# A w_out product by seven products of half-size blocks, with feed-forward groups of two chunks

## The chip, the core and the metric

The kernel runs on one core of a Trainium2 chip. Its engines each work through a queue of their own: PE (TensorE) multiplies matrices, DVE (VectorE) and ACT (ScalarE) do elementwise work, POOL (GpSimd) fills tiles at the start, and SP (SyncE) issues the DMAs. The metric is the device time of one execution in microseconds (us); less is better. The profile shows one execution, with times from the start of its span.

## What is computed

A gated linear attention over 4 batches, 8 heads, 768 steps and head size 48, and then a feed-forward block with SiLU on its 3072 rows of 384:

```
state = alpha[:, :, t, :, None] * state + einsum('bhd,bhe->bhde', k[:, :, t], v[:, :, t])
y[:, :, t] = einsum('bhd,bhde->bhe', q[:, :, t], state)
...
x = y.transpose(0, 2, 1, 3).reshape(3072, 384)
h = x @ w_in                       # w_in  384 x 2048
g = h * (1.0 / (1.0 + exp(-h)))
out = (g @ w_out).astype(float32)  # w_out 2048 x 384
```

q, k, v and alpha are float32; w_in and w_out arrive as float64. All matmuls of the kernel are float32.

## The kernel before

**Chunks and steps.** The sequence is cut into 24 chunks (6 stretches of 128 steps, 4 batches each). A chunk goes through five stages: `products` (transposes of alpha, k and q on PE; running products of alpha by two scans on DVE; k times one of them gives `kp`, q times the other gives `qp`), `scores` (matmuls of kp and qp into `g`, masked on DVE; transposes of kp), `values` (g times v, and qp times the carried state), `bridge` (the chunk's output, transposed, goes into a tile `xt`) and `states` (the new carried state). A loop of 27 steps calls the five stages for five successive lags, and after each stage `fill` puts in some feed-forward work.

**Feed-forward.** `moe(ci)` takes the four chunks of a stretch, 512 tokens. For each of 16 slices of w_in's columns three matmuls of 512 columns go into a PSUM tile `ps_m` (two buffers), and ACT applies SiLU into a tile `g`. Then for each of the four chunks 16 matmuls of 384 columns add up g times w_out, ACT copies the result and SP stores it. These are 32 pieces to a stretch; `fill` hands them out at an even pace from step FIRST = 7 on, and a stretch may begin once its four chunks are bridged.

**Weights.** They come as float64 words: a DMA brings a piece into `bits` (four buffers), ACT scales the low words, and three DVE instructions (L464, L465, L466) put float32 together. There are 12 pieces of w_in (converted before step 7) and 16 of w_out (converted beside the first stretch). Later `audit` reads alpha and the weights again and reduces them on DVE (L499), to confirm the bounds on which the arithmetic rests; the program takes another path only if they fail.

**Order.** A scheduler places the instructions of each engine by its own estimate of times, so the order on an engine is not quite that of the code. Each engine then works strictly through its order.

Of the kernel before, what the change touches and what calls it, by code (L numbers as in the profile page):

```python
# [8 lines left out]
F32 = mybir.dt.float32  # L9
# [321 lines left out]
def quotients(  # L331
# [30 lines left out]
    W = C + 1  # L362

# [12 lines left out]
    gpool = pool("gpool", NFT + 3)  # L376
    opool = pool("opool", 2)
    ps_t = pool("ps_t", 3, PS)
# [6 lines left out]
    NIN = 4  # L385
# [10 lines left out]
    def load(n):  # L396
        ci, b = divmod(n, B)
        c = ctxs[n] = {"ci": ci, "b": b}
        rows = slice(ci * C, ci * C + C)
        for name, src in (("a", alpha), ("k", k), ("q", q)):  # L400
            c[name] = nat[name][n % NIN]
            nc.sync.dma_start(c[name][:, :, 0:D], src[b, :, rows, :].transpose([1, 0, 2]))
        c["v"] = vpool.tile([128, H, D], F32, name="vn")
        nc.sync.dma_start(c["v"], v[b, :, rows, :].transpose([1, 0, 2]))
# [31 lines left out]
    w_out = wpool.tile([128, NFT, HD], F32, name="w_out")  # L436
    for n in range(2, NIN):
        load(n)

    wide = moe_w_in.dtype != F32  # L440

    def weights(which):

        pieces = [
            (w_in[:, t, c : c + 512], moe_w_in[t * 128 : t * 128 + 128, c : c + 512])
            for c in range(0, DF, 512) for t in range(NKT)
        ] if which == 0 else [  # L450
            (w_out[:, f, :], moe_w_out[f * 128 : f * 128 + 128, :]) for f in range(NFT)]
        for dst, src in pieces:
# [12 lines left out]
            dve.scalar_tensor_tensor(w, hi, -(1 << 30), w, ALU.bitwise_and, ALU.bitwise_or)  # L465
            dve.tensor_tensor(w, w, up, ALU.add)  # L466
            yield
# [41 lines left out]
    def products(n):  # L509
# [11 lines left out]
        u = work.tile([128, end + 1], F32, name="u")  # L521
        dve.tensor_tensor_scan(u[:, end - 1 :: -1], sg[:, end:0:-1], one[:, end:0:-1],  # L522
                               0.0, ALU.mult, ALU.add)
        kp = c["kp"] = work.tile([128, NP, C], F32, name="kp")
        dve.tensor_tensor(kp, ps["k"], tokens(u), ALU.mult)  # L525
# [3 lines left out]
        p = work.tile([128, end + 1], F32, name="p")  # L529
        dve.tensor_tensor_scan(p[:, 0:end], sg[:, 0:end], iv[:, 0:end], 0.0, ALU.mult, ALU.add)  # L530
        qp = c["qp"] = work.tile([128, NP, C], F32, name="qp")
        dve.tensor_tensor(qp, ps["q"], tokens(p), ALU.mult)  # L532
# [57 lines left out]
    def bridge(n):  # L590
        c = ctxs.pop(n)
        ci, b = c["ci"], c["b"]
        if b == 0:
            xts[ci] = xtp.tile([128, NKT, B * C], F32, name="xt")
# [4 lines left out]
        act.copy(xts[ci][:, :, b * C : (b + 1) * C], ps)  # L599

    def moe(ci):

        xt = xts.pop(ci)
        gs = []
        for f in range(NFT):
            ps = ps_m.tile([128, B * C], F32, name="ps_m")
            for t in range(NKT):
                pe.matmul(ps, lhsT=w_in[:, t, f * 128 : (f + 1) * 128], rhs=xt[:, t, :],  # L608
                          start=(t == 0), stop=(t == NKT - 1))
            gf = gpool.tile([128, B * C], F32, name="g")  # L610
            act.activation(gf, ps, AF.Silu)  # L611
            gs.append(gf)
            yield
        for b in range(B):
            ps = ps_m.tile([128, HD], F32, name="ps_m")
            for f in range(NFT):
                pe.matmul(ps, lhsT=gs[f][:, b * C : (b + 1) * C], rhs=w_out[:, f, :],  # L617
                          start=(f == 0), stop=(f == NFT - 1))
                if f % 4 == 3 and f < NFT - 1:
                    yield  # L620
            o = opool.tile([128, HD], F32, name="o")
            act.copy(o, ps)  # L622
            r = b * S + ci * C
            nc.sync.dma_start(out[r : r + C, :], o)
            yield

    PIECES = NFT + 4 * B
# [9 lines left out]
    def ffn():  # L637
        for ci in range(NCH):
            yield from moe(ci)
# [5 lines left out]
    total = NCH * PIECES  # L645
    STEPS = NT + 3
    FIRST = B + 3
    SLOTS = 5

    def fill(step, slot):  # L650

        nonlocal done
        if step < FIRST:
            if step >= 1:
                convert(0, ((step - 1) * SLOTS + slot + 1) * n_conv[0] // ((FIRST - 1) * SLOTS))
            return
        if step > FIRST + 2 and slot in (0, 2):
# [7 lines left out]
    for step in range(STEPS):  # L665
        for slot, (stage, lag) in enumerate(
# [6 lines left out]
            if stage is states and 0 <= n and n + NIN < NT:  # L673
                load(n + NIN)
# [9 lines left out]
    if wide:  # L684
        checks += [(seen[1][0], ALU.max, float(1150 << 20), ALU.is_le),
# [64 lines left out]
```

## Time and profile before

| | us |
|---|---|
| median of 3 runs (lowest to highest) | 691.74 (691.45 to 692.13) |
| the profiled execution | 691.06 |
| its span, first to last instruction | 689.3 |
| PE busy | 668.8 |
| DVE busy | 227.3 |
| ACT busy | 132.6 |
| mean granted PE clock | 0.992 of full |

The span is what the profile's times refer to; the execution's own time is 1.8 us longer. The busy time of an engine is the union of its instructions, so those that overlap count once. A line number such as L617 is that of the kernel's source. `ps_m<-w_out,g` means that the instruction writes ps_m and reads w_out and g, with buffer numbers left out. Time in square brackets, or after a bar in the groups, is idle time of the engine ahead of the instructions, with what ended it.

### The profile page before, as it was taken

Reading aid. Unit: us, or ns where it says so; the run is one execution under the profiler, and the core shown is the slowest. Engines: PE = TensorE matmul, PEld = TensorE weight load, DVE = VectorE, ACT = ScalarE, POOL = GpSimd, SP = SyncE. Lnnn points to the kernel's source line nnn. Section 1 sums busy time; section 2 is a strip of 40 time slices with the busy share of each in tenths; the row PEclk is TensorE's granted clock in tenths of the full one; section 3 lists DMA queues with packets and bytes.
Section 4 is the critical chain, followed back from the end, with each engine's and each line's share of the span. In section 5 each row is a group of like instructions: output and inputs, shape, how many; then the busy total and the mean of one; then the engine's idle time right before and its main releaser. Section 6 shows DMA issues by size and latency. Waiting matters only on the chain.

```text
span 689.3 us, 7061 instructions
## 1 busy us (share of the span) xinstructions
PE 668.8 (97%) x2874; PEld 410.9 (60%) x2874; DVE 227.3 (33%) x414; ACT 132.6 (19%) x242; POOL 6.2 (1%) x27
## 2 busy tenths in 40 slices
PE   6889999999999999999999999999999999999996
PEld 4786545666455666645666844566854456644553
DVE  4999986878130221303020600213440001000000
ACT  1423642001222101222100222110122100122100
POOL 3000000000000000000000000000000000000000
PEclk9979999999999999999999999999999999999999
DMA  9998799899020230302020500200100000000000
GB/s 158 247 223 210 224 232 307 263 291 278 18 36 17 41 57 12 58 0 47 20 49 23 92 1 0 42 27 24 28 8 1 0 23 12 14 1 1 11 12 28
DMA packets 112698, 54.04 MB, mean 78 GB/s; under 512 B 101264, under 2 KB 104336, under 8 KB 112656
## 3 DMA queue, kind: packets, MB, share of 16 engines
q1 hardware_dynamic: 112656, 53.49, 33.1%
q8 instruction: 25, 0.41, 0.2%
q14 instruction: 17, 0.14, 0.1%
HBM read 48.76 MB, written 4.72 MB: 78 GB/s over the span
## 4 chain that ended last, share of the span: by engine, by line
PE 85%; DMA 2%; DVE 1%; ACT 1%; issue 0%; ACTq 0%; SPq 0%
PE ps_m L617 36%; PE ps_m L608 33%; PE ps_y L563 5%; PE ps_t L517 3%; PE ps_g L543 3%; PE ps_y L568 2%; PE ps_y L580 2%; DMA bits<-in_moe_w_out_dram 2%; PE ps_t L551 1%; PE ps_t L598 1%; DVE w_out L466 0%; DVE w_out L465 0%; ACT x L572 0%; DVE u L522 0%; ACT g L611 0%
## 5 line engine op out<-in xcount | busy, mean ns | idle before, releaser
L617 PE MATMUL ps_m<-w_out,g 128*128 128x384 f32 x768 | 255.0, 487 | 0.0
L608 PE MATMUL ps_m<-xt,w_in 128*128 128x512 f32 x576 | 251.7, 594 | 1.6 <-ACT g L611 1.1
L617 PEld LDWEIGHTS ps_m<-w_out,g 128*128 128x128 f32 x768 | 143.1, 190 | 92.9 <-issue 1.9
L608 PEld LDWEIGHTS ps_m<-xt,w_in 128*128 128x128 f32 x576 | 107.6, 190 | 129.7 <-issue 126.2
L611 ACT ACTIVATE g<-ps_m 128x512 f32<-128x512 f32 x96 | 57.2, 596 | 180.2 <-PE ps_m L608 180.2
L586 DVE TENSOR_TENSOR st<-ps_y,st 48x192 f32<-48x192 f32 x32 | 11.3, 354 | 144.2 <-PE ps_y L580 143.9
L563 PEld LDWEIGHTS ps_y<-vn,g 128*128 128x128 f32 x384 | 47.6, 198 | 5.7 <-issue 1.9
L563 PE MATMUL ps_y<-vn,g 128*128 128x48 f32 x384 | 47.8, 278 | 0.6 <-DVE st L588 0.3
L522 DVE TENSOR_TENSOR_SCAN u<-al,one 128x516 f32<-128x516 f32 x24 | 29.5, 1230 | 52.4 <-ACT al L519 52.0
L499 DVE TENSOR_REDUCE seen<-bits 128x1 f32<-128x384 int32 (+2 forms) x65 | 42.2, 687 | 12.7 <-DMA bits<-in_moe_w_out_dram 5.4
L547 DVE TENSOR_TENSOR g<-ps_g,mask 128x512 f32<-128x512 f32 x48 | 31.3, 682 | 30.6 <-PE ps_g L543 30.5
L622 ACT COPY o<-ps_m 128x384 f32<-128x384 f32 x24 | 11.5, 479 | 153.5 <-PE ps_m L617 121.3
L525 DVE TENSOR_TENSOR kp<-ps_t,u 128x512 f32<-128x512 f32 x24 | 16.6, 690 | 63.4 <-PE ps_t L517 61.4
L532 DVE TENSOR_TENSOR qp<-ps_t,p 128x512 f32<-128x512 f32 x24 | 16.5, 686 | 59.3 <-PE ps_y L568 59.2
L543 PEld LDWEIGHTS ps_g<-qp,kp 48*128 48x128 f32 x384 | 24.5, 195 | 13.4 <-issue 8.8
L543 PE MATMUL ps_g<-qp,kp 48*128 48x128 f32 x384 | 29.4, 294 | 2.9 <-DVE qp L532 2.9
L530 DVE TENSOR_TENSOR_SCAN p<-al,inv 128x516 f32<-128x516 f32 x24 | 29.5, 1229 | 0.5
L572 ACT COPY x<-ps_y 128x384 f32<-128x384 f32 x24 | 11.5, 479 | 79.5 <-PE ps_y L568 73.3
L580 PEld LDWEIGHTS ps_y<-vn,kn 128*128 128x128 f32 x160 | 21.4, 198 | 7.2 <-ACT x L572 3.4
L553 ACT COPY kn<-ps_t 128x512 f32<-128x512 f32 x20 | 11.7, 587 | 62.0 <-PE ps_t L551 62.0
L517 PE MATMUL ps_t<-ident,an 128*128 128x128 f32 x96 | 17.9, 300 | 5.9 <-POOL one L420 4.1
L580 PE MATMUL ps_y<-vn,kn 128*128 128x96 f32 x160 | 23.0, 285 | 0.5 <-ACT x L572 0.2
(53 smaller groups left out, 278.0 us busy)
## 6 DMA issues: line engine op xcount, KB each, us to landing
bits<-in_moe_w_in_dram SPq DMA_DIRECT2D x24, 512.0 KB, 5.0
bits<-in_moe_w_out_dram SPq DMA_DIRECT2D x32, 384.0 KB, 4.2
an<-in_alpha_dram SPq DMA_DIRECT2D x24, 192.0 KB, 4.6
kn<-in_k_dram SPq DMA_DIRECT2D x24, 192.0 KB, 4.9
qn<-in_q_dram SPq DMA_DIRECT2D x24, 192.0 KB, 4.9
vn<-in_v_dram SPq DMA_DIRECT2D x24, 192.0 KB, 2.7
bits<-in_alpha_dram SPq DMA_DIRECT2D x9, 512.0 KB, 5.2
out_dram<-o SPq DMA_DIRECT2D x24, 192.0 KB, 1.9
```

Of the source, the lines that this page charges most:

```text
L499: dve.tensor_reduce(seen[kind][which][:, i : i + 1], x, axis=AX, op=op, apply_absolute_value=True)
L517: pe.transpose(ps[name][:, j, :], c[name][:, 2 * j : 2 * j + 2, :], ident)
L522: dve.tensor_tensor_scan(u[:, end - 1 :: -1], sg[:, end:0:-1], one[:, end:0:-1], 0.0, ALU.mult, ALU.add)
L525: dve.tensor_tensor(kp, ps["k"], tokens(u), ALU.mult)
L530: dve.tensor_tensor_scan(p[:, 0:end], sg[:, 0:end], iv[:, 0:end], 0.0, ALU.mult, ALU.add)
L543: pe.matmul(ps[:, u, j, :], lhsT=c["kp"][r, j, :], rhs=c["qp"][r, j, :], start=True, stop=True)
L547: dve.tensor_tensor(g[:, u], ps[:, u], mask[:, None, :].to_broadcast([128, NP, C]), ALU.mult)
L563: pe.matmul(py[:, h, :], lhsT=g[:, h % 2, h // 2, :], rhs=vn[:, h, :], start=(h == 0), stop=(ci == 0 and h == H - 1), skip_group_check=True)
L580: pe.matmul(ps[:, j], lhsT=c["kn"][:, j, :], rhs=vn[:, 2 * j : 2 * j + 2, :], start=True, stop=True)
L608: pe.matmul(ps, lhsT=w_in[:, t, f * 128 : (f + 1) * 128], rhs=xt[:, t, :], start=(t == 0), stop=(t == NKT - 1))
L611: act.activation(gf, ps, AF.Silu)
L617: pe.matmul(ps, lhsT=gs[f][:, b * C : (b + 1) * C], rhs=w_out[:, f, :], start=(f == 0), stop=(f == NFT - 1))
```

## The change

The feed-forward part now takes groups of two chunks (256 tokens), twelve in all, of 15 pieces each. The w_in product is done as before with matmuls of 256 columns, two slices to a ps_m tile.

The w_out product is treated as one of 2x2 blocks: the rows of g are the two chunks, its columns the even and odd slices of 128, and the columns of w_out are two halves of 192. Instead of eight block products it makes seven, from sums and differences of blocks: `s1` to `s4` are made of g by DVE for every group, `t1`, `t2`, `t4` and a changed b12 of w_out once, when its pieces are converted (`differences`). The four output blocks are put together from the seven products partly by adding up in PSUM (px, py, pv) and partly on DVE (u2, u3 and three of four stores). Each product is 8 matmuls of 192 columns.

kp and qp are written over the running products instead of tiles of their own, and buffers are dealt out anew (the gpool tiles are larger and fewer, `up` has a pool of two). There are three input sets instead of four; the loads of a, k and q are issued from `products`, v's two chunks ahead. `fill` starts at step 5 with 8 of the 12 w_in pieces converted; the rest come between the first pieces of feed-forward work.

```
-    gpool = pool("gpool", NFT + 3)
+    gpool = pool("gpool", HF // 2 + 1)
+    spool = pool("spool", HF // 2)
...
+    upool = pool("upool", 2)
+    ppool = pool("ppool", 3)
...
-    NIN = 4
+    NIN = 3
...
+    blocks = w_out.rearrange("p (i k) (c n) -> p k i c n", k=2, c=2)
+    (b11, b12), (b21, b22) = [[blocks[:, k, :, c, :] for c in range(2)] for k in range(2)]
+    wt = wpool.tile([128, 3, HF, HO], F32, name="wt")
+    t1, t2, t4 = [wt[:, i] for i in range(3)]
...
+    def differences(i):
+        dve.tensor_tensor(t1[:, i], b12[:, i], b11[:, i], ALU.subtract)
+        dve.tensor_tensor(t2[:, i], b22[:, i], t1[:, i], ALU.subtract)
+        dve.tensor_tensor(t4[:, i], b21[:, i], t2[:, i], ALU.subtract)
+        dve.tensor_tensor(b12[:, i], b22[:, i], b12[:, i], ALU.subtract)
...
-            up = gpool.tile([128, 512], I32, name="g")[:, 0:n]
+            up = upool.tile([128, 512], I32, name="up")[:, 0:n]
...
+            if which and at % 4 == 3:
+                differences(slice(at // 2 - 1, at // 2 + 1))
...
-        kp = c["kp"] = work.tile([128, NP, C], F32, name="kp")
-        dve.tensor_tensor(kp, ps["k"], tokens(u), ALU.mult)
+        kp = c["kp"] = u[:, 1 : end + 1].rearrange("p (j c) -> p j c", c=W)[:, :, 0:C]
+        dve.tensor_tensor(kp, ps["k"], kp, ALU.mult)
...
-        qp = c["qp"] = work.tile([128, NP, C], F32, name="qp")
-        dve.tensor_tensor(qp, ps["q"], tokens(p), ALU.mult)
+        qp = c["qp"] = tokens(p)
+        dve.tensor_tensor(qp, ps["q"], qp, ALU.mult)
...
+        for i in range(HF):
+            ps = ps_m.tile([128, 2, GB * C], F32, name="ps_m")
+            for e in range(2):
+                f = 2 * i + e
+                for t in range(NKT):
+                    pe.matmul(ps[:, e, :], lhsT=w_in[:, t, f * 128 : (f + 1) * 128], rhs=xt[:, t, :],
+                              start=(t == 0), stop=(t == NKT - 1))
+            if i % 2 == 0:
+                gf = gpool.tile([128, 2, 2, 2, C], F32, name="g")
+            act.activation(gf[:, i % 2], ps, AF.Silu)
+            if i % 2 == 1:
+                sf = spool.tile([128, 4, 2, C], F32, name="s")
+                a11, a12, a21, a22 = [gf[:, :, e, m, :] for m in range(2) for e in range(2)]
+                s1, s2, s3, s4 = [sf[:, j] for j in range(4)]
+                dve.tensor_tensor(s1, a21, a22, ALU.add)
+                dve.tensor_tensor(s2, s1, a11, ALU.subtract)
+                dve.tensor_tensor(s3, a11, a21, ALU.subtract)
+                dve.tensor_tensor(s4, a12, s2, ALU.subtract)
...
+        def product(ps, name, w, first=False):
+            for i in range(HF):
+                pe.matmul(ps, lhsT=a[name][i], rhs=w[:, i, :], start=(first and i == 0),
+                          stop=(i == HF - 1), skip_group_check=True)
...
+        px = acc()
+        product(px, "11", b11, True)
+        act.copy(u1, px)
+        yield
+        py = acc()
+        product(py, "s2", t2, True)
+        dve.tensor_tensor(u2, py, u1, ALU.add)
+        yield
+        product(px, "12", b21)
+        store(0, 0, px)
+        yield
+        product(py, "s3", b12)
+        dve.tensor_tensor(u3, py, u1, ALU.add)
+        yield
+        pv = acc()
+        product(pv, "s1", t1, True)
+        store(1, 1, pv, u3)
+        yield
+        product(py, "22", t4)
+        store(1, 0, py, u1)
+        yield
+        product(pv, "s4", b22)
+        store(0, 1, pv, u2)
...
-    FIRST = B + 3
+    FIRST = GB + 3
...
-                convert(0, ((step - 1) * SLOTS + slot + 1) * n_conv[0] // ((FIRST - 1) * SLOTS))
+                convert(0, ((step - 1) * SLOTS + slot + 1) * 8 // ((FIRST - 1) * SLOTS))
...
-        share = total * ((step - FIRST) * SLOTS + slot + 1) // (SLOTS * (STEPS - FIRST))
-        while done < share and done // PIECES * B + B <= bridged:
+        share = total * ((step - FIRST) * SLOTS + slot + 1) // (SLOTS * (STEPS - FIRST + 1))
+        while done < share and done // PIECES * GB + GB <= bridged:
+            convert(0, 3 * (done // 2) + 6)
             convert(1, 2 * done + 2)
```

How the instructions stand on an engine is shown at two places; the numbers behind the x count repeats of the program's own instructions, and a matmul counts once here. In the changed source L547 and L582 are the transposes that were L517 and L551, L574 the scores (L543), L594 and L599 the values (L563, L568), L611 the states (L580), L629 the bridge (L598), L642 the w_in product (L608) and L662 the w_out product (L617).

On PE, before, the passage in which the first w_out matmuls come; chunks 6 and 7 are in their stages in between:

```order
L608 MATMUL ps_m<-xt,w_in 128x512 x18
L543 MATMUL ps_g<-qp,kp 128x128 x6
L551 MATMUL ps_t<-ident,kp 128x128 x4
L563 MATMUL ps_y<-vn,g 128x48 x4
L608 MATMUL ps_m<-xt,w_in 128x512 x12
L563 MATMUL ps_y<-vn,g 128x48 x4
L568 MATMUL ps_y<-st_153,qp 128x96 x4
L608 MATMUL ps_m<-xt,w_in 128x512 x6
L598 MATMUL ps_t<-ident,x 128x128 x3
L608 MATMUL ps_m<-xt,w_in 128x512 x3
L617 MATMUL ps_m<-w_out,g 128x384 x4
```

The same passage on PE in the changed kernel, with wt the differences of w_out and s the sums of g:

```order
L547 MATMUL ps_t<-ident,an_109 128x128
L547 MATMUL ps_t<-ident,kn_115 128x128 x4
L642 MATMUL ps_m<-xt,w_in 128x256 x10
L662 MATMUL ps_m<-w_out,g 128x192 x6
L662 MATMUL ps_m<-wt,s 128x192 x6
L662 MATMUL ps_m<-w_out,g 128x192 x9
L662 MATMUL ps_m<-wt,s 128x192 x2
L662 MATMUL ps_m<-w_out,g 128x192
L574 MATMUL ps_g<-p,u 128x128
```

The first w_out matmuls now follow 48 matmuls of 256 columns rather than 48 of 512, and the scores of chunk 6 stand behind them.

On DVE, before, the end of the conversion of w_out (L464 to L466 are its three instructions):

```order
L556 TENSOR_TENSOR st_151<-st_151,u 128x384
L528 RECIPROCAL inv_139<-least 128x4
L464 TENSOR_SCALAR w_out<-bits 128x384
L530 SCALAR_TENSOR_TENSOR p<-al_137,inv_139 128x516
L465 SCALAR_TENSOR_TENSOR w_out<-bits,w_out 128x384
L464 TENSOR_SCALAR w_out<-bits 128x384
L466 ISA w_out<-w_out,g 128x768
L465 SCALAR_TENSOR_TENSOR w_out<-bits,w_out 128x384
L547 TENSOR_TENSOR g<-ps_g,mask 128x512
L466 ISA w_out<-w_out,g 128x768
```

The same place on DVE in the changed kernel, where L492 to L494 are the conversion, L463 to L466 the differences and L651 to L654 the sums:

```order
L653 TENSOR_TENSOR s<-g 128x256
L654 TENSOR_TENSOR s<-g,s 128x256
L492 TENSOR_SCALAR w_out<-bits 128x384 x2
L493 SCALAR_TENSOR_TENSOR w_out<-bits,w_out 128x384 x2
L494 ISA w_out<-w_out,up 128x768 x2
...
L463 TENSOR_TENSOR wt<-w_out 128x384
L651 TENSOR_TENSOR s<-g 128x256
L464 TENSOR_TENSOR wt<-w_out,wt 128x384
L466 TENSOR_TENSOR w_out<-w_out 128x2x192
L465 TENSOR_TENSOR wt<-w_out,wt 128x384
L652 TENSOR_TENSOR s<-s,g 128x256
```

Attention work has left this stretch of DVE's queue, and the differences and sums have come into it.

More of the change, by code (lines that the diff above doesn't have):

```diff
@@ L362, in quotients @@
     W = C + 1
+    GB = 2
+    NG = NT // GB
+    HF = NFT // 2
+    HO = HD // 2
     def pool(name, bufs=1, space=None):
@@ L402, in load, with load_v @@
             nc.sync.dma_start(c[name][:, :, 0:D], src[b, :, rows, :].transpose([1, 0, 2]))
+    def load_v(n):
+        c = ctxs[n]
+        rows = slice(c["ci"] * C, c["ci"] * C + C)
         c["v"] = vpool.tile([128, H, D], F32, name="vn")
-        nc.sync.dma_start(c["v"], v[b, :, rows, :].transpose([1, 0, 2]))
+        nc.sync.dma_start(c["v"], v[c["b"], :, rows, :].transpose([1, 0, 2]))
     load(0)
@@ L466, in weights @@
             dve.tensor_tensor(w, w, up, ALU.add)
+            if which and at % 4 == 3:
+                differences(slice(at // 2 - 1, at // 2 + 1))
             yield
@@ L598, in bridge @@
             pe.transpose(ps[:, t, :], xf[:, t * 128 : (t + 1) * 128], ident)
[L599 to L612, printed above, removed]
-            yield
[L614 to L622, printed above, removed]
-            r = b * S + ci * C
-            nc.sync.dma_start(out[r : r + C, :], o)
-            yield
@@ L637, in ffn @@
     def ffn():
-        for ci in range(NCH):
-            yield from moe(ci)
+        for grp in range(NG):
+            yield from moe(grp)
     filler, audits = ffn(), audit()
     done, bridged = 0, 0
-    total = NCH * PIECES
+    total = NG * PIECES
     STEPS = NT + 3
-    FIRST = B + 3
+    FIRST = GB + 3
     SLOTS = 5
@@ L672, in quotients @@
                     bridged = n + 1
-            if stage is states and 0 <= n and n + NIN < NT:
-                load(n + NIN)
+                if stage is products and n + NIN < NT:
+                    load(n + NIN)
+                if stage is products and n + 2 < NT:
+                    load_v(n + 2)
             fill(step, slot)
```

39 lines of the change are left out of this document (30 added, 9 removed).

## The prediction

> **What bounds the kernel now.** I read the page first: busy shares and the forty slices.
>
> ```profile
> span 689.3 us, 7061 instructions
> PE 668.8 (97%) x2874; PEld 410.9 (60%) x2874; DVE 227.3 (33%) x414; ACT 132.6 (19%) x242; POOL 6.2 (1%) x27
> ...
> PE   6889999999999999999999999999999999999996
> ...
> DVE  4999986878130221303020600213440001000000
> ```
>
> PE is full from the fifth slice on; in the first six DVE is full instead, and PE has holes. So there are two stages with different limits. Next the groups of instructions with shapes kept apart, for what fills PE:
>
> ```profile
> L617 PE MATMUL ps_m<-w_out,g 128*128 128x384 f32 x768 | 255.0, 487 | 0.0
> L608 PE MATMUL ps_m<-xt,w_in 128*128 128x512 f32 x576 | 251.7, 594 | 1.6 <-ACT g L611 1.1 <-ACT xt L599 0.4
> L568 PEld LDWEIGHTS ps_y<-st,qp 128*128 128x128 f32 x160 | 19.5, 192 | 0.0
> ```
>
> The feed-forward part is 507 of 669 us. Each matmul of the program is two records (384 of 128x384 are written, 768 recorded), so counts below are records. The mean of one (487 ns) holds the latency; the pace is read from the timeline of PE, start to start:
>
> ```profile
> 591.88 1.16 PE L543 MATMUL ps_g<-qp,kp 48*128 48x128 f32 x16
> 592.97 1.99 PE L563 MATMUL ps_y<-vn,g 128*128 128x48 f32 x16
> 594.79 1.10 PE L568 MATMUL ps_y<-st,qp 128*128 128x96 f32 x8
> 595.72 0.49 PE L598 MATMUL ps_t<-ident,x 128*128 128x128 f32 x3
> ...
> 601.11 41.47 PE L608 MATMUL ps_m<-xt,w_in 128*128 128x512 f32 x96 [0.45 <-ACT xt L599]
> 605.94 0.59 PE L608 MATMUL ps_m<-xt,w_in 128*128 128x512 f32 x1
> 605.94 0.19 PEld L608 LDWEIGHTS ps_m<-xt,w_in 128*128 128x128 f32 x1 [0.24 <-issue]
> 642.42 41.44 PE L617 MATMUL ps_m<-w_out,g 128*128 128x384 f32 x128
> ```
>
> The second column is the time from the first start to the last end. Dense paces: 512 columns (642.42-601.11)/96 = 430.3 ns; 384 columns about 41.3/128 = 322.8 ns (the last record's drain taken off); 96 columns (595.72-594.79)/8 = 116 ns; 48 columns 1.82/16 = 114 ns; the 48x128 scores 1.09/16 = 68 ns. At the wide end cost goes with columns, 0.840 ns each and 0.3 ns over; at the narrow end it stops falling near 115 ns, the pace of a 128-column weight load.
>
> The start, by stretches and on the timeline:
>
> ```profile
> 7.28:100.10 92.82, 83.21 (x501) 60.86 (x501) 87.27 (x170) 35.71 (x66) 0.00 (x0) 0.94 1.03 221
> 100.10:200.00 99.90, 99.88 (x412) 59.76 (x411) 61.39 (x105) 16.73 (x31) 0.00 (x0) 1.00 0.74 214
> 200.00:600.00 400.00, 399.29 (x1724) 245.27 (x1723) 78.05 (x136) 65.97 (x123) 0.00 (x0) 1.00 0.13 26
> ```
>
> Columns are length, then busy time of PE, weight load, DVE, ACT, POOL, then granted clock, DMA share, GB/s. From DVE's first scan (7.28) to its last conversion of w_out (100.10) DVE works 87.27 of 92.82 us, and PE's clock is at 0.94. After that PE never waits.
>
> **The change part by part.**
>
> *Narrower matmuls in the w_in product.* 576 records of 512 columns become 1152 of 256. The line through 384 and 512 gives 215.3 ns; a fixed cost of 3 ns on a pure column price gives 216.3. I take 215.5: 1152 x 215.5 = 248.3 us against 576 x 430.3 = 247.9. Cost +0.4, range 0 to +4 (218.5 each).
>
> *Seven products for eight.* Per group of two chunks 7 x 8 matmuls of 192 columns, twelve groups, two records: 1344 for 768 of 384. The line gives 161.5; I take 162.5, which lies nearest to the wide rows since 162 is well over the 114 to 116 at which the narrow rows stop. 1344 x 162.5 = 218.4 against 768 x 322.8 = 247.9: -29.5. Upper bound from the nearest narrow row, whose 96 columns would be 81 ns on the line and took 116: a price 35 over the line, 197 ns, and then +17. What could make it so is the weight load, of which there are now 2496 for 1344; L568 shows that loads lasting 192 ns follow each other every 116, so they overlap one another, and I keep the line.
>
> The Trainium skill, "TensorE: Matmul & The Clock Gate", section "The mechanism", says that a weight load overlaps matmuls in flight only when its row group differs; all of these use the same rows. This case's trace disagrees: 48 and 96 columns take the same 114 to 116, which load and matmul in series could not. By that rule the time would be 957 us (worked out from rows in rival 3); by the trace the term is -29.5.
>
> *Feed-forward sum: -29.1 us* on an engine that is full after 100 us.
>
> *The sums of blocks on DVE.* Per group 16 sums of 128x256, then 2 intermediate results and 3 outputs of 128x192 read from PSUM; ACT makes 2 copies of 192 for 2 of 384.
>
> ```profile
> L465 DVE SCALAR_TENSOR_TENSOR w_out<-bits,w_out 128x384 int32<-128x384 int32 x16 | 8.7, 547 | 0.0
> L465 DVE SCALAR_TENSOR_TENSOR w_in<-bits,w_in 128x512 int32<-128x512 int32 x12 | 8.1, 676 | 0.0
> L586 DVE TENSOR_TENSOR st<-ps_y,st 48x192 f32<-48x192 f32 x32 | 11.3, 354 | 144.2 <-PE ps_y L580 143.9
> L556 DVE TENSOR_TENSOR st<-st,u 128x384 f32<-128x384 f32 x20 | 10.9, 547 | 0.0
> L522 DVE TENSOR_TENSOR_SCAN u<-al,one 128x516 f32<-128x516 f32 x24 | 29.5, 1230 | 52.4 <-ACT al L519 52.0
> L530 DVE TENSOR_TENSOR_SCAN p<-al,inv 128x516 f32<-128x516 f32 x24 | 29.5, 1229 | 0.5
> L525 DVE TENSOR_TENSOR kp<-ps_t,u 128x512 f32<-128x512 f32 x24 | 16.6, 690 | 63.4 <-PE ps_t L517 61.4 <-PE ps_g L543 0.5
> L532 DVE TENSOR_TENSOR qp<-ps_t,p 128x512 f32<-128x512 f32 x24 | 16.5, 686 | 59.3 <-PE ps_y L568 59.2
> L547 DVE TENSOR_TENSOR g<-ps_g,mask 128x512 f32<-128x512 f32 x48 | 31.3, 682 | 30.6 <-PE ps_g L543 30.5
> ```
>
> 547 at 384 and 676 at 512 make 418 at 256: 192 x 0.418 = 80 us, and 60 x 0.354 = 21 us. With 16 differences of w_out blocks at 547 (8.8 us) DVE goes from 227 to about 337 us, half of the span. After the start this is beside PE: an intermediate result has a whole other product, 16 x 162.5 = 2.6 us, before PE needs its bank again. If DVE is late there, PE waits at once, since ps_m has two buffers; I carry 2 us for the stage from 100 to 200 us, where the audits run (the reductions of L499): DVE had 61.39 us of 99.90 there, and two groups' sums and results, 2 x 8.5 us, make it 78. The bounds are 0 and 8.
>
> *Scaled k and q in place.* Same operations, fewer tiles: 0. Cover: none needed. Rows of 129 words shift the operands; L563 reads v at offsets of 48 words at 114 ns like the rest, so I give it nothing.
>
> *The start, the term that speaks against.* Before, w_out is first needed after 48 matmuls of 512 columns (117 us on the timeline); now after one small group, and the order puts it ahead of attention work that PE used to do first. In the new order of the program PE comes to the last pieces of w_out after 147 transposes, 48 score, 40 value, 20 state and 4 carry matmuls, and 48 + 12 of the feed-forward part. By the paces above (transposes 110 ns, from the three rows below; state matmuls like the carry ones), with two records for all but transposes, that is 16.2 + 6.5 + 9.1 + 4.6 + 0.9 + 20.7 + 3.9 = 61.9 us of full-speed work. DVE must by then have made: all conversions, as before; attention for two chunks less (2 x (1.230 + 0.690 + 1.229) + 0.686 + 4 x 0.682 + 2 x 0.547 + 4 x 0.354 = 12.2 us off); 12 sums and 12 differences (5.0 + 6.6 on). So DVE's last conversion stays where it is:
>
> ```profile
> 4.12 1.09 PE L517 MATMUL ps_t<-ident,an 128*128 128x128 f32 x4 [4.12 <-POOL one L420]
> ...
> 35.29 1.16 PE L543 MATMUL ps_g<-qp,kp 48*128 48x128 f32 x16 [2.73 <-DVE qp L532]
> ...
> 97.18 10.57 PE L608 MATMUL ps_m<-xt,w_in 128*128 128x512 f32 x24
> 99.55 0.55 DVE L466 CUSTOM_DVE_ANT_0 w_out<-w_out,g 128x768 uint16<-128x768 uint16 x1
> ...
> 117.43 2.74 PE L617 MATMUL ps_m<-w_out,g 128*128 128x384 f32 x8
> ...
> 126.06 0.60 PE L517 MATMUL ps_t<-ident,an 128*128 128x128 f32 x4
> 126.50 0.60 PE L517 MATMUL ps_t<-ident,kn 128*128 128x128 f32 x4
> ...
> 34.00:52.00 18.00, 15.81 (x105) 14.14 (x105) 16.40 (x32) 5.43 (x11) 0.00 (x0) 0.72 1.07 220
> ```
>
> 100.10 - 0.6 = 99.5 us, of which PE has used 61.9: 37.6 lost. Before, PE at 100.1 has done by the same paces 108 + 32 + 15 transposes, 64 score, 52 value, 24 state and 8 carry matmuls, and 61 records of w_in: 17.1 + 8.7 + 11.9 + 5.6 + 1.9 + 26.2 = 71.4; 28.7 lost. The change loses 9 us more. Below: DVE loses its 5.6 idle us, and the first transposes, which waited 4.12 us for POOL, start 1 us earlier with three fills fewer ahead of them: 7 us better, +2. Above: its idle time doubles, since PE now holds feed-forward work ahead of what DVE waits for, +15. After the hole of 2.73 us at 35.29 the clock fell to 0.72 over 18 us; one such spell in dense work after 99 us costs up to 5. I take 1.5.
>
> *DMA and the end.* Loads go out from the products stage, v behind the weights; out_dram goes as 48 halves. Both are off PE after 100 us. The last output is 192 columns on DVE (354) for 384 on ACT; 0.
>
> *Sum*, against the profiled execution, 691.06 us (span 689.3): 691.06 - 29.1 + 9 + 1.5 + 2 = 674.5. It ran 0.7 under the median of 691.74, so I say 675.
>
> **The rivals.**
>
> 1. The weight load binds the 192-column matmuls. L608's loads start with the matmul ahead of them and last 190; if that holds at 192 columns, each costs 192 ns: 1344 x 29.5 = 40 us more, 715, slower. It decides from 162.5 + 16.7/1344, that is 175 ns on. For: load time above matmul time. Against: L568, a load each 116 ns.
>
> 2. DVE becomes the bound through the whole kernel: each group's five results come 0.3 us late, and PE stands. 60 x 0.3 = 18 us, 693, no change. For: the stage 100 to 200, where DVE has 61.39 us already and gets 16 sums and 5 results for each 55 us or so of PE's. Against: 200 to 600 has 78.05 us in 400.
>
> 3. Load and matmul run in series. From 48 columns, a load is at most 114: 1344 x (114 + 161) + 1152 x (114 + 215) - 496 = 253 us for -29.1, that is 957. Against it: 96 columns would then take 114 + 81 and take 116, and 384 would take 437 and take 323. This is what the page's rule would give.
>
> 4. The start costs nothing more, since DVE fills its holes: 666. For: its 5.6 us. Against: the counts above.
>
> **How the numbers follow.** 675 with its own range 663 to 687 (start +2 to +15, columns +4, audits 0 to 8): chance 0.72. Rival 4: 0.12. Rival 2, in part or whole: 0.08. Rival 1: 0.06. Rival 3: 0.02. The range 662 to 689 leaves out rivals 1 and 3, half of 2 and a tail of the likeliest, under 0.2. Faster takes the first two, and a third of rival 2: 0.87; within 0.2% (1.4 us, what a measurement of this kernel can tell) 0.03; slower 0.10.
>
> **What would show it.** The new PE groups: 1344 x 192 columns with busy time near 219 us (rival 1: 258), 1152 x 256 near 249. DVE near 335 us. PE waiting on w_out, w_in or sums between 60 and 100 us, and full from about 100. If PE's idle time after 200 us is over 5 us and ends with DVE, rival 2; if PE is full by 85 us, rival 4. The forecast is wrong if 192 columns cost 175 ns or more, or the start loses over 25 us more.

## The result, and the profile after

| | before | changed |
|---|---|---|
| median, us (lowest to highest; runs) | 691.6 (691.45 to 692.13; 4) | 674.0 (669.01 to 676.57; 4) |
| the profiled execution, us | 691.06 | 675.27 |
| ratio of the times, 95% interval | | 0.9735, 0.9676 to 0.9795 |

The changed kernel is 2.6% faster, by 17.6 us; 675 us was forecast. Two later sets of runs gave ratios of 0.9743 (0.9707 to 0.978) and 0.976 (0.9731 to 0.979). One execution of a later experiment (pieces ahead, timed again) took 956.62 us at a granted clock of 0.651; its ratio leaves it out, and without it that median is 670.80. The page of the changed kernel, with the same parts as shown of before:

```profile
span 673.5 us, 9767 instructions
PE 646.3 (96%) x4026; PEld 597.7 (89%) x4026; DVE 326.4 (48%) x682; ACT 129.2 (19%) x242; POOL 5.7 (1%) x24
...
PE   6899579999999999999999999999999999999996
...
DVE  5989998898733524434245154161352441121120
...
PEclk9979798999999999999999999999999999999999
```

A slice is 16.8 us. The fifth and sixth slices of PE (67 to 101 us) have sunk to 5 and 7 tenths, and DVE is full in both; the granted clock dips in the third, fifth and seventh. From the seventh slice on PE is full again. From the twelfth on DVE, mostly at 0 to 3 tenths before, is mostly at 1 to 5.

The paces are read, as before, from PE's timeline of the last group, start to start:

```profile
628.84 20.99 PE L642 MATMUL ps_m<-xt,w_in 128*128 128x256 f32 x96 [0.45 <-ACT xt L630]
649.67 2.76 PE L662 MATMUL ps_m<-w_out,g 128*128 128x192 f32 x16
652.27 2.76 PE L662 MATMUL ps_m<-wt,s 128*128 128x192 f32 x16
...
665.27 2.76 PE L662 MATMUL ps_m<-w_out,s 128*128 128x192 f32 x16
```

256 columns take (649.67 - 628.84)/96 = 217.0 ns, and 192 columns 2.60/16 = 162.5 ns. The passage at the start, again on PE's timeline:

```profile
75.04 6.53 PE L642 MATMUL ps_m<-xt,w_in 128*128 128x256 f32 x16 [5.11 <-DVE w_in L494]
...
96.82 0.59 PE L662 MATMUL ps_m<-w_out,g 128*128 128x192 f32 x2 [1.35 <-DVE w_out L494]
99.24 1.01 PE L662 MATMUL ps_m<-w_out,g 128*128 128x192 f32 x2 [1.82 <-DVE w_out L494]
100.66 4.49 PE L662 MATMUL ps_m<-w_out,g 128*128 128x192 f32 x14 [0.41 <-ACT u L681]
...
109.56 2.44 PE L662 MATMUL ps_m<-wt,s 128*128 128x192 f32 x14
```

PE waits for the conversion of w_in (5.11 us) and of w_out (twice), and gets the last piece of w_out that it waits for at 99.24 us. The 14 matmul records from 100.66 then take 4.49 us, where 14 of the same shape at 109.56 take 2.44: that is the half clock behind the waits (granted clock 0.50 from 100 to 104 us). The stretches (length, busy time of PE, weight load, DVE, ACT, POOL, then granted clock, DMA share, GB/s):

```profile
0.00:60.00 60.00, 52.16 (x333) 45.77 (x334) 46.79 (x87) 19.20 (x32) 5.75 (x24) 0.91 1.04 182
60.00:100.00 40.00, 28.65 (x164) 23.84 (x162) 39.74 (x90) 16.96 (x32) 0.00 (x0) 0.89 0.95 261
100.00:150.00 50.00, 49.59 (x286) 45.66 (x286) 45.30 (x84) 6.21 (x12) 0.00 (x0) 0.95 0.76 249
150.00:200.00 50.00, 48.87 (x307) 45.37 (x307) 32.47 (x75) 9.45 (x18) 0.00 (x0) 1.00 0.49 141
200.00:600.00 400.00, 399.50 (x2566) 373.46 (x2565) 149.27 (x315) 67.55 (x129) 0.00 (x0) 1.00 0.16 31
```

The second of them in the kernel before:

```profile
60.00:100.00 40.00, 38.81 (x178) 22.47 (x178) 38.36 (x83) 19.57 (x36) 0.00 (x0) 1.00 0.90 223
```

From 60 to 100 us DVE works 39.74 of 40 us, and PE stands 11 us instead of 1. After 200 PE's idle time is 0.5 us in 400, with nearly twice as much DVE work beside it as before (149.27 for 78.05).

### The profile page after: what moved, and what is told of

It reads as the page before. It is cut to its first block, busy times and chain, and to the rows that moved or that the text cites. A ratio compares the mean times of both kernels' runs of the same rounds, so it can differ in the third digit from the quotient of the medians.

```text
span 673.5 us, 9767 instructions
## 1 busy us (share of the span) xinstructions
PE 646.3 (96%) x4026; PEld 597.7 (89%) x4026; DVE 326.4 (48%) x682; ACT 129.2 (19%) x242; POOL 5.7 (1%) x24
## 4 chain that ended last, share of the span: by engine, by line
PE 81%; DVE 11%; DMA 4%; issue 1%; ACT 1%; SPq 0%; ACTq 0%; DVEq 0%
PE ps_m L642 32%; PE ps_m L662 29%; PE ps_y L594 5%; PE ps_t L547 4%; PE ps_g L574 4%; DVE seen L529 3%; PE ps_y L599 2%; PE ps_y L611 2%; DMA bits<-in_moe_w_out_dram 2%; PE ps_t L582 2%; DMA bits<-in_moe_w_in_dram 2%; PE ps_t L629 1%; DVE w_out L494 1%; DMA an<-in_alpha_dram 1%; DVE u L552 1%
## 5 line engine op out<-in xcount | busy, mean ns | idle before, releaser
L642 PE MATMUL ps_m<-xt,w_in 128*128 128x256 f32 x1152 | 261.6, 383 | 5.9 <-DVE w_in L494 5.1
L642 PEld LDWEIGHTS ps_m<-xt,w_in 128*128 128x128 f32 x1152 | 216.9, 192 | 35.1 <-DVE w_in L494 5.3
L651 DVE TENSOR_TENSOR s<-g 128x256 f32<-128x256 f32 x48 | 20.3, 422 | 144.1 <-ACT g L646 143.9
L662 PE MATMUL ps_m<-w_out,g 128*128 128x192 f32 x384 | 69.6, 335 | 3.6 <-DVE w_out L494 3.2
L662 PEld LDWEIGHTS ps_m<-w_out,g 128*128 128x128 f32 x384 | 64.8, 196 | 5.0 <-DVE w_out L494 3.8
L662 PE MATMUL ps_m<-wt,s 128*128 128x192 f32 x384 | 66.9, 327 | 0.0
L662 PE MATMUL ps_m<-w_out,s 128*128 128x192 f32 x384 | 66.6, 327 | 0.0
L662 PEld LDWEIGHTS ps_m<-wt,s 128*128 128x128 f32 x384 | 62.5, 190 | 0.2 <-ACT o L672 0.2
L662 PEld LDWEIGHTS ps_m<-w_out,s 128*128 128x128 f32 x384 | 62.5, 190 | 0.1
L594 PEld LDWEIGHTS ps_y<-vn,g 128*128 128x128 f32 x384 | 48.0, 198 | 1.2 <-ACT x L603 0.5
L594 PE MATMUL ps_y<-vn,g 128*128 128x48 f32 x384 | 47.4, 277 | 0.3 <-ACT x L603 0.3
L552 DVE TENSOR_TENSOR_SCAN u<-al,one 128x516 f32<-128x516 f32 x24 | 29.5, 1230 | 29.4 <-ACT al L549 29.3
L662 PE MATMUL ps_m<-wt,g 128*128 128x192 f32 x192 | 33.3, 327 | 0.9 <-DVE u L691 0.9
L574 PEld LDWEIGHTS ps_g<-p,u 48*128 48x128 f32 x384 | 25.2, 199 | 8.2 <-issue 6.2
L662 PEld LDWEIGHTS ps_m<-wt,g 128*128 128x128 f32 x192 | 31.2, 190 | 1.1 <-DVE u L691 1.1
L574 PE MATMUL ps_g<-p,u 48*128 48x128 f32 x384 | 30.2, 297 | 1.7 <-DVE p L563 1.7
L561 DVE TENSOR_TENSOR_SCAN p<-al,inv 128x516 f32<-128x516 f32 x24 | 29.5, 1229 | 0.5
```

Of the source, the lines that this page charges most:

```text
L574: pe.matmul(ps[:, u, j, :], lhsT=c["kp"][r, j, :], rhs=c["qp"][r, j, :], start=True, stop=True)
L594: pe.matmul(py[:, h, :], lhsT=g[:, h % 2, h // 2, :], rhs=vn[:, h, :], start=(h == 0), stop=(ci == 0 and h == H - 1), skip_group_check=True)
L642: pe.matmul(ps[:, e, :], lhsT=w_in[:, t, f * 128 : (f + 1) * 128], rhs=xt[:, t, :], start=(t == 0), stop=(t == NKT - 1))
L651: dve.tensor_tensor(s1, a21, a22, ALU.add)
L662: pe.matmul(ps, lhsT=a[name][i], rhs=w[:, i, :], start=(first and i == 0), stop=(i == HF - 1), skip_group_check=True)
```

## The experiments

Each is the changed kernel with one edit, timed beside the kernel before on the same chip. Ratios are to that kernel, whose own median was 691.6 to 693.5 us in the four sets, so ratios compare better across sets than medians.

| what | median, us | ratio, 95% interval |
|---|---|---|
| narrower still (one run) | 619.78 | |
| eight products of 384 columns | 689.05 | 0.9962, 0.9935 to 0.9989 |
| no sums and differences | 664.42 | 0.959, 0.9566 to 0.9613 |
| w_out's conversion cut to a third | 660.77 | 0.9544, 0.9521 to 0.9566 |
| differences and first sums on POOL | 684.39 | 0.9885, 0.9857 to 0.9914 |
| dummy matmuls in the waits | 673.64 | 0.9728, 0.9701 to 0.9755 |
| next group's w_in product ahead | 670.81 | 0.9682, 0.9645 to 0.972 |
| the same, timed again | 670.84 | 0.9694, 0.9666 to 0.9722 |
| the changed kernel, beside "no sums", "dummy" and "ahead" | 676.07 | 0.9743, 0.9707 to 0.978 |
| the changed kernel, beside "timed again" | 676.18 | 0.976, 0.9731 to 0.979 |

### What a matmul of 96 to 192 columns costs

```
+        WIDE = {"11": 96, "12": 96, "s2": 128, "s3": 128, "22": 128, "s1": 160, "s4": 160}
...
-                pe.matmul(ps, lhsT=a[name][i], rhs=w[:, i, :], start=(first and i == 0),
+                n = HO if first and i == 0 else WIDE[name]
+                pe.matmul(ps[:, 0:n], lhsT=a[name][i], rhs=w[:, i, 0:n], start=(first and i == 0),
```

> The changed kernel with all but the first matmul of each PSUM bank cut short in columns: 96 columns for the products 11 and 12, 128 for s2, s3 and 22, 160 for s1 and s4 (the other columns of these are left out). It measures the pace of a matmul of 128x128 weights between 96 and 192 columns. Theory (cost is the larger of 0.84 ns a column and the pace of a weight load): 96 columns 112 to 116 ns, 128 columns 112 to 117, 160 columns 134 to 137. Rival (a load that lasts 190 ns begins with the matmul ahead of it): 190 or more for all three.

Measured, on PE's timeline of the last two groups (rows in which all 16 matmuls have one width: 160, then 96, 128, 128 and 160 columns):

```profile
574.98 2.34 PE L665 MATMUL ps_m<-w_out,s 128*128 128x160 f32 x16
577.15 0.49 PE L629 MATMUL ps_t<-ident,x 128*128 128x128 f32 x3
...
602.81 1.92 PE L665 MATMUL ps_m<-w_out,g 128*128 128x96 f32 x16
604.57 1.98 PE L665 MATMUL ps_m<-w_out,s 128*128 128x128 f32 x16
...
608.61 1.95 PE L665 MATMUL ps_m<-wt,g 128*128 128x128 f32 x16
610.39 2.34 PE L665 MATMUL ps_m<-w_out,s 128*128 128x160 f32 x16
```

96 columns: (604.57 - 602.81)/16 = 110 ns. 128: (610.39 - 608.61)/16 = 111. 160: (577.15 - 574.98)/16 = 135.6. The first two lie 1 to 2 ns under the range that was expected. So cost follows columns (135.6/160 = 0.847 ns each) down to about 130, and stands at 110 ns for 96 and 128, while a weight load of these products lasts 191 to 198 ns in the mean. 192 columns are well above that floor: rivals 1 (192 ns) and 3 (about 275) fall.

### Eight products in the new order

```
-        (the sums s1 to s4, the differences, the seven products)
+        for m in range(GB):
+            ps = ps_m.tile([128, 512], F32, name="ps_m")[:, 0:HD]
+            for f in range(NFT):
+                pe.matmul(ps, lhsT=gs[f][:, m, :], rhs=w_out[:, f, :],
+                          start=(f == 0), stop=(f == NFT - 1))
```

> The changed kernel with the w_out product done plainly: groups of two chunks as in the changed kernel, matmuls of 256 columns for w_in, but 2 x 16 matmuls of 384 columns for w_out, no sums, no differences, and ACT copying the results. Theory (the gain is the narrower products alone, less what the start pays): PE pays 768 x 322.8 = 247.9 us for w_out instead of 218.4, so +29.5 on the changed kernel's 674; DVE has 11.6 us less ahead of its last conversion of w_out, which gives back up to 11. So 690, between 685 and 700, the kernel before within 1%. Rival (the gain comes from the smaller groups and the earlier start of the feed-forward part): 680 or less.

Measured: 689.05, 2.9 us under before. Groups of two chunks, the other buffers, the other places of the loads and the in-place k and q together are worth about that much (0.1 to 0.65% by the interval). On PE's timeline the first w_out product has nothing to wait for:

```profile
84.79 20.93 PE L648 MATMUL ps_m<-w_out,g 128*128 128x384 f32 x64
```

Its 64 records (32 matmuls) run through w_out twice in 20.9 us, and no sum or difference stands ahead of a conversion on DVE. The seven products bring the rest, 13 us by the medians (689.05 to 676.1) or 15 by the ratios (0.9962 to 0.9743), of 29.5 us less work on PE.

### No sums and differences

```
+    t1, t2, t4 = b12, b22, b21
...
+                s1, s2, s3, s4 = a21, a22, a11, a12
```

> The changed kernel with all sums of g and all differences of w_out left out: the seven products multiply blocks as they are (the result is wrong), while the five results of each group stay. DVE has 89 us less to do, 11.6 of it ahead of its last conversion. Theory (DVE's sums cost only in the start; after 110 us they are beside PE): 8 to 12 us gained, 662 to 666, and PE's idle time after 200 us unchanged. Rival (the sums hold PE up in every group): 658 or less.

Measured: 664.42, 11.65 us under the changed kernel beside it (676.07). The stretches, first of this kernel, then of the changed one in the same set:

```profile
60.00:100.00 40.00, 34.26 (x234) 29.17 (x232) 37.99 (x82) 17.56 (x34) 0.00 (x0) 0.96 0.89 251
...
200.00:600.00 400.00, 399.49 (x2543) 372.88 (x2542) 98.77 (x185) 69.03 (x131) 0.00 (x0) 1.00 0.15 29
```

```profile
60.00:100.00 40.00, 28.15 (x140) 23.96 (x140) 38.94 (x90) 17.12 (x32) 0.00 (x0) 0.87 0.97 277
...
200.00:600.00 400.00, 399.50 (x2555) 373.25 (x2552) 146.17 (x311) 68.73 (x131) 0.00 (x0) 1.00 0.15 30
```

From 200 to 600 us, 47 us less of DVE work changes PE's busy time by 0.01. So the sums cost nothing there, and rival 2 falls. They cost at the start: with them gone PE is busy 34.26 of 40 us instead of 28.15, at a clock of 0.96 instead of 0.87.

### A third of w_out's conversion

```
+            if which == 0:
                 dve.scalar_tensor_tensor(w, hi, -(1 << 30), w, ALU.bitwise_and, ALU.bitwise_or)
                 dve.tensor_tensor(w, w, up, ALU.add)
```

> The changed kernel with two of the three DVE instructions that convert a piece of w_out left out (the values of w_out are then wrong); its DMAs and ACT's part stay. Theory (DVE's queue sets when the last piece of w_out is ready, and PE stands for it): 16 x (0.547 + 0.549) = 17.5 us less on DVE ahead of that point, which then comes at 82 to 85 us instead of 99; the time falls by 12 to 17 us, to 657 to 662. Rival (w_out's DMAs, of which the last are issued from 85 to 92 us, set it): the last piece still comes after 92 us, and the time falls by 5 us or less, 669 or more.

Measured: 660.77, as the theory had it. The place of the last piece was a miss. PE's timeline and stretch:

```profile
92.67 0.59 PE L663 MATMUL ps_m<-w_out,g 128*128 128x192 f32 x2 [0.36 <-DVE w_out L492]
```

```profile
60.00:100.00 40.00, 35.41 (x242) 31.15 (x240) 37.19 (x83) 18.38 (x35) 0.00 (x0) 1.00 0.91 253
```

w_out's last awaited piece came 6.6 us earlier than in the changed kernel's first profile, not 14 or more, and after 92 us, as the rival had it. That rival's time (669 or more) did not come, and DVE stood for a DMA of w_out only once, for 0.5 us, so the DMAs are not what PE waits for. The rest of the gain came by another way: in the order that the scheduler gave this kernel, chunk 6's scores stand ahead of the end of w_out, and PE had them to do meanwhile (35.41 us busy where it was 28.65), at full clock. DVE's busy time fell by 15.0 us (326.4 to 311.4), and the median by 13 to 15 (from 674.0 or 676.1). In the kernel without sums DVE had 76.3 us less to do (326.3 to 250.0), of which the prediction counted 11.6 into the start, and the gain was 11.65. That they agree so closely is luck: sums start 0.33 us apart on DVE, differences 0.47, so the 12 of each ahead of that point take about 9.6 us of its time, and like profiles (below) give a gain of 10.0. Together this says what DVE's time is worth here: a microsecond of it before 100 us is roughly one microsecond of the kernel (0.8 to 1.2), and after 200 us it is worth nothing. Since both edits moved the scheduler's order too, the price is that of the two together.

### Differences and first sums on POOL

```
-        dve.tensor_tensor(t1[:, i], b12[:, i], b11[:, i], ALU.subtract)
+        gps.tensor_tensor(t1[:, i], b12[:, i], b11[:, i], ALU.subtract)
...
+                vec = gps if grp == 0 else dve
+                vec.tensor_tensor(s1, a21, a22, ALU.add)
```

> The changed kernel with the 16 differences of w_out, and the 16 sums of the first group alone, moved from DVE to POOL, which is idle there. Theory (as before, DVE's queue): 11.6 us less on DVE ahead of its last conversion, so 8 to 11 us gained, 663 to 666. Rival 1 (the DMAs set it): 669 or more. Rival 2 (POOL is so much slower at these that PE waits for the first group's sums and for the last differences instead): 674 or more, with PE idle ahead of products of wt or s, ended by POOL.

Measured: 684.39, which by the ratios is 9 to 10 us slower than the changed kernel; 8 to 11 us of gain were expected. The groups of this kernel (busy time, mean ns of one):

```profile
L493 DVE SCALAR_TENSOR_TENSOR w_out<-bits,w_out 128x384 int32<-128x384 int32 x16 | 12.4, 776 | 0.0
L492 DVE TENSOR_SCALAR w_out<-bits 128x384 int32<-128x384 int32 x16 | 8.7, 546 | 0.0
L465 POOL TENSOR_TENSOR wt<-w_out,wt 128x384 f32<-128x384 f32 x4 | 5.1, 1268 | 0.0
```

and the same operations in the changed kernel, all on DVE:

```profile
L493 DVE SCALAR_TENSOR_TENSOR w_out<-bits,w_out 128x384 int32<-128x384 int32 x16 | 8.6, 549 | 0.0
L492 DVE TENSOR_SCALAR w_out<-bits 128x384 int32<-128x384 int32 x16 | 5.4, 353 | 0.0
L465 DVE TENSOR_TENSOR wt<-w_out,wt 128x384 f32<-128x384 f32 x4 | 2.2, 548 | 0.0
```

A difference takes 1268 ns on POOL for 548 on DVE, and DVE's own conversions lengthen in the mean from 549 to 776 and from 353 to 546 ns. What was moved off DVE came back as longer instructions; PE's last wait for w_out ended later and was longer:

```profile
102.30 1.01 PE L663 MATMUL ps_m<-w_out,g 128*128 128x192 f32 x2 [4.26 <-DVE w_out L494]
```

This profile is of the fastest of the four runs (678.33), 3.06 us over the first profile of the changed kernel (675.27), and the wait ends 3.06 us later (102.30 for 99.24). The other three took 683 to 686, two of them at a granted clock of 0.969, so a part of the 9 to 10 us may be the clock. Rival 2 had the time (674 or more) but not the place: no wait of PE ends with POOL.

### Dummy matmuls in the waits

```
+    zero = consts.tile([128, 128], F32, name="zero")
+    dve.memset(zero, 0.0)
...
+            if grp == 0 and i == 4:
+                warm(ps[:, 0, 0:HO], 14, True)
...
+                if grp == 0 and name == "11" and i >= 6:
+                    warm(ps, 5)
```

> The changed kernel with 24 matmuls of a zero tile in the places of the first group where PE stood (14 ahead of its fifth piece, 5 each ahead of the last two matmuls of its first product); they add nothing to the result. The order around them shifts a little, since the scheduler counts their time. Theory (after each wait of the start PE works at half clock for a spell; the one at 97 to 105 us falls on dense work): the spells between 70 and 105 us go, the granted clock rises from 0.981 to 0.99 or more, and 3 to 5 us are gained, 669 to 671, with less spread. Rival (the spells cost nothing, since DVE sets the pace): 674 with a higher clock, or more, by the 8 us of added matmuls.

`warm` adds zero times a piece of w_in to the accumulation. Measured: 673.64, 2.4 us under the changed kernel beside it, with overlapping intervals. From 84 to 100 us the clock was at 1.00 instead of the 0.89 of the changed kernel in the same set, and over the whole runs at 0.985 to 0.990, where three of four of the changed kernel had 0.978 to 0.982. A higher clock at about 674 us is what the rival had, but the dummies take PE's time, and the order around them moved as well. So this one is inconclusive; no effect beyond these 2.4 us was seen.

### The changed kernel again, and where its scatter comes from

> The changed kernel as it is, beside the other three on the same chip: 669 to 677, with a spread of several us from run to run that goes with the granted clock (lower clock, longer time).

> The changed kernel, unchanged, as the control for the order with pieces ahead: 674 to 677 by both readings.

Over the three sets the 14 runs of the changed kernel fall in two groups: five with a mean granted clock of 0.989 to 0.992 took 669.0 to 672.7 us, and nine at 0.978 to 0.983 took 675.3 to 678.4. Two profiles, one of each, show how a small loss of clock becomes 4.5 us. The first is the one above, 675.27 us; here are DVE's row and the stretch in which its clock fell:

```profile
42.57 0.35 DVE L619 COPY st<-ps_y 48x192 f32<-48x192 f32 x1 [3.01 <-PE ps_y L611]
...
34.00:44.00 10.00, 10.00 (x56) 9.68 (x55) 6.89 (x14) 3.90 (x7) 0.00 (x0) 0.54 1.14 225
```

The other took 670.74 us; its copy at the same place, its first 60 us, and its last wait for w_out on PE:

```profile
38.85 0.32 DVE L619 COPY st<-ps_y 48x192 f32<-48x192 f32 x1
...
0.00:60.00 60.00, 51.25 (x369) 43.60 (x369) 50.45 (x93) 19.64 (x33) 5.77 (x24) 1.00 1.08 195
...
95.45 0.59 PE L662 MATMUL ps_m<-w_out,g 128*128 128x192 f32 x2 [1.82 <-DVE w_out L494]
```

At half clock PE's state matmuls (L611) come late, and DVE, which works strictly in order, stands 3.01 us at the copy with conversions queued behind it. By 60 us it has done 46.79 us of work instead of 50.45, 3.7 less, and w_out's last piece is 3.8 us later (99.24 for 95.45). The kernel is 4.5 us longer. The clock costs here by way of DVE, before 60 us, more than in the matmuls after 100.

The same spell of half clock stands in other profiles of this document. In seven the clock is 0.50 to 0.55 from 34 to 44 us, and DVE works 6.9 to 7.4 of these 10 us; in the other four with the new order it is 1.00, and DVE works 9.8 to 9.9. So part of a difference between two kernels can be this draw, and profiles are best compared within a kind, though each is one execution and runs of one kind scatter by 3 to 4 us. With the spell, against 675.27: 665.28 without sums, 669.60 and 669.49 with pieces ahead (next section), 675.92 with dummies, 678.33 with POOL. Without it, against 670.74: 658.24 with the short conversion, 688.03 with eight products. So 10.0 us for the sums, 12.5 for the conversion, 5.7 to 5.8 for the pieces ahead, nothing for the dummies, 3.1 lost by POOL and 17.3 for seven products instead of eight.

### Half of the next group's w_in product ahead of each group's products

```
+            part = first(grp)
+            for i in range(HF):
+                if i == HF // 2 and grp > 0:
+                    yield from second(grp - 1)
+                next(part)
+                yield
...
-            convert(1, 2 * done + 2)
+            convert(1, (4 * done + 4) // 3 + 1)
```

`first` makes a group's eight pieces of g, `second` the seven products; the sums of a group are made beside the next group's first pieces. gpool has six tiles.

> The changed kernel with the first half of the next group's w_in pieces placed ahead of each group's seven products (gpool of 6 for 5, ppool of 2 for 3), so that the first product comes 24 matmuls of 256 columns, 10.4 us of PE work, later in PE's order; the conversion of w_out is spread over 12 pieces instead of 8. Theory (what PE lacks at 90 to 99 us is work that doesn't need w_out): 6 to 10 us gained, 664 to 668. Rival (the work put ahead waits itself for DVE, since chunks 2 and 3 must be through their attention first): 672 or more.

> The order with half of the next group's w_in pieces ahead of each group's products, timed again in more rounds beside the changed kernel itself. If what it wins is the wait for w_out at the start, it stays about 5 us below the changed kernel (669 to 672 against 674 to 677) and the intervals of the two ratios come apart; the rival is that the 5 us were the draw of half-clock spells, and then both lie within 2 us.

Measured: 670.81 and 670.84. In the second set the intervals come apart (0.9722 and 0.9731): 5.3 us faster than the changed kernel, in place of the 6 to 10 of the first expectation. The rows of the second set, PE's timeline and stretch:

```profile
71.80 5.41 PE L655 MATMUL ps_m<-xt,w_in 128*128 128x256 f32 x16 [1.46 <-DVE w_in L494]
79.19 1.13 PE L655 MATMUL ps_m<-xt,w_in 128*128 128x256 f32 x4 [1.98 <-DVE w_in L494]
...
99.30 0.59 PE L673 MATMUL ps_m<-w_out,g 128*128 128x192 f32 x2 [0.65 <-DVE w_out L494]
```

```profile
60.00:100.00 40.00, 34.80 (x193) 29.40 (x192) 39.20 (x89) 18.28 (x35) 0.00 (x0) 0.96 0.93 269
```

PE is busy 34.80 of these 40 us instead of 28.65: the second group's w_in matmuls fill the wait for w_out. What is left are the waits for w_in itself at 70 to 82 us, which this order does not touch, and DVE is still busy 39.20 of 40 us there. This is the best version found that has all of the work in it, 0.969 of before.

## Why the prediction was right

| step | as predicted | as measured |
|---|---|---|
| 256 columns | 215.5 ns, +0.4 us | 217.0 ns, +2.1 us |
| 192 columns | 162.5 ns, -29.5 us | 162.5 ns, -29.5 us |
| the last piece of w_out that PE waits for | 99.5 us | 99.24 us |
| the start and the clock | +9 and +1.5 us | +10.1 us, what is left |
| idle PE, 100 to 200 us | +2 us | +1.5 us |
| the profiled execution | 674.5 us | 675.27 us |

- **The paces.** Both come from rows above. The 256 columns cost 1.5 ns more than taken: 1152 x 1.5 = 1.7 us, inside its bounds. The busy times named as signs came out higher, 236.4 us for the four groups of 192 columns (near 219 was forecast) and 261.6 for 256 (near 249). They hold the last record's latency of each product (2.76 us for 16 x 162.5 ns = 2.60, 84 times, 13.4 us) and the half-clock matmuls of the start, so the paces decide here.
- **The start.** It is the difference of the two profiled executions, -15.8 us, less the feed-forward part's -27.4 and the 1.5 us of idle time. By the count of work itself 99.24 - 61.9 = 37.3 us are lost against 28.7, so 8.6, and about 2 more are the half-clock matmuls at 100.66. That DVE is what sets it is shown from both sides: less DVE work in the start gave 10 to 11.65 us (no sums) and 12.5 to 15 (short conversion), stretched DVE work cost 3 to 10 (POOL). Each of these edits also moved the scheduler's order, which no run holds fixed.
- **Where it was luck.** The 99.24 us is that of a profile with the half-clock spell at 34 us; in the run of 670.74 us the same piece came at 95.45. The profile before, from which the 99.5 was taken, has such a spell too (0.72 from 34 to 52 us), so the two agree by the draw of the profiled run. And the range of 663 to 687 is not the plain sum of the bounds given for the start, the clock, the 256 columns and the idle time, which is 664 to 694; the result lies well inside both.
- **The waits' places.** They ended with DVE's w_in and w_out, as forecast. The longest, 5.11 us, was for w_in, for which the prediction had no term of its own; its count of work up to the last piece of w_out took it in.
- **DVE's sums.** 335 to 337 us of busy time were forecast and 326.4 came. The step that failed is the price of each sum: 418 ns is how long one lasts, and I used it as what it occupies. On DVE's timeline:

```profile
54.48 0.42 DVE L651 TENSOR_TENSOR s<-g 128x256 f32<-128x256 f32 x1
54.81 0.42 DVE L653 TENSOR_TENSOR s<-g 128x256 f32<-128x256 f32 x1
55.14 0.42 DVE L652 TENSOR_TENSOR s<-s,g 128x256 f32<-128x256 f32 x1
```

  One starts every 0.33 us. Leaving out all 192 sums and 16 differences took 76.3 us of busy time off DVE, for the 89 forecast. It did not move the time, since most of it lies under PE.
- **The lower bound of the start.** Of "1 us earlier for the first transposes" nothing came: on PE's timeline the first one still starts at 4.03 us, now waiting for the DMA of alpha.
- **The clock.** The size was right (+1.5 taken, bounds 0 to 5), the way was another. I put the spell into the dense matmuls after 99 us; there it cost 2. Its larger effect is at 34 us, by way of DVE, and accounts for most of the 4.5 us between the two profiles. Whether it makes the whole scatter of 9 us (669.0 to 678.4), two profiles cannot say.
- **The rivals.** 1 and 3 fall by the narrow matmuls; with 3 falls, for these float32 matmuls, the rule of the Trainium skill that it followed ("TensorE: Matmul & The Clock Gate", "The mechanism"), since they all use the same rows and loads of 191 to 198 ns stand beside matmuls that start 110 ns apart. 2 falls by the equal stretches from 200 to 600 us. 4 falls by PE's 28.65 of 40 us.

## What to carry to other kernels

Cutting PE's work pays in full only where PE sets the pace: of 29.5 us saved on the w_out product, 10 to 16 went back at the start, where DVE had just been given the sums and PE's need for the converted weights came earlier. Price such a change in each stage by the engine that is full there, and count how much work the others have ahead of the piece that they will wait for. Work of a later group placed ahead of that piece won 5 us; moving DVE's work to POOL lost 3 us in like profiles and 9 to 10 by the ratios.

## What the hardware showed that I had not expected

- **DVE and POOL.** DVE's instructions grew by 1.4 to 1.55 times in the mean in the run with work on POOL (549 to 776 ns, 353 to 546), but not evenly: the median of the 16 instructions of L493 stayed at 551 ns, and the longest took 1352. The Trainium skill, "SBUF — State Buffer", section "SBUF: two separate sides", says that the two share a pair of ports which one holds for a whole instruction while the other waits (against DVE instructions in a two-port mode or with two SBUF inputs). Single instructions of this run agree with that. On POOL's timeline:

```profile
83.03 6.91 POOL L652 TENSOR_TENSOR s<-g 128x256 f32<-128x256 f32 x1 [0.92 <-ACT g L646]
89.90 1.03 POOL L654 TENSOR_TENSOR s<-g 128x256 f32<-128x256 f32 x1
```

  The first lasts 6.91 us where others like it last about 1, and beside it DVE runs its conversions at their usual lengths. From 92.76 to 103.5 us, while POOL works without a pause, each conversion of w_out on DVE takes 0.88 to 1.35 us instead of 0.35 to 0.55. Which of DVE's instructions are in a two-port mode no run shows.
- **Short waits and the clock.** PE's wait for `p` in one chunk's scores, in the changed kernel, in its run of 670.74 us, and in the kernel with eight products:

```profile
33.10 2.08 PE L574 MATMUL ps_g<-p,u 48*128 48x128 f32 x16 [1.67 <-DVE p L563]
```

```profile
32.47 1.16 PE L574 MATMUL ps_g<-p,u 48*128 48x128 f32 x16 [1.44 <-DVE p L563]
```

```profile
32.85 1.16 PE L570 MATMUL ps_g<-p,u 48*128 48x128 f32 x16 [1.67 <-DVE p L559]
```

  In the first the 16 matmuls take 2.08 us and the clock stands at 0.54 from 34 to 44 us; in the others they take 1.16, and it stays at 1.00, though one of the waits is as long. The Trainium skill, "TensorE: Matmul & The Clock Gate", section "What's actually happening", lets the clock fall after an idle window of about 3.4 us. The wait of the first case falls well short of that, and PE works 4.04 of the 6 us from 28 to 34. The same wait of 1.67 or 1.68 us stands in nine profiles of this document, and in seven of them the spell at half clock follows. What decides between the cases stays open.
- **The floor of a narrow float32 matmul.** It is 110 to 111 ns per record for 96 and for 128 columns, beside weight loads that last 191 to 198 ns each.
